# Attention over mixture memory, then an expert layer, on one core: first keys and queries through SyncE, both score parities in one step, 4096-byte stores

## The chip, the cores and the metric

One core of one Trainium2 chip. The metric is the device time of the kernel in microseconds. Of the engines, PE is TensorE (its weight loads are listed apart as PEld), DVE is VectorE, ACT is ScalarE, POOL is GpSimd and SP is SyncE. DMAs that POOL issues form the "software" queue, those that SP issues the "hardware" queue; both run on the core's 16 DMA engines.

## The reference

```
q, k, v: [8, 8, 576, 64] (batch, head, position, head_dim);  phi: [8, 8, 576, 32];  all f32
a      = softmax of phi over its 32 memories
k_m    = sum over positions of a * k      (32 x 64 for each batch and head);  v_m likewise with v
scores = q k_m^T / 8;  attn = softmax of scores over the 32 memories;  out = attn v_m
x      = out as [4608, 512]: a row is a position of a batch, heads side by side
y      = max(x w1_dense, 0) w2_dense                             (512 -> 512 -> 512)
       + gate * max(x w1[e], 0) w2[e],  e = argmax of x w_gate over 8 experts,  gate = softmax's value at e
```

The output is [4608, 512] f32.

## The kernel before, in words

The kernel works through eight batches of 576 rows. All matmuls are f16 with f32 sums in PSUM. Its 128 partitions hold a pair of heads (`a` is the parity of the head, `p` a position group of 64), so a tile such as `q` or `kv` has four pairs `j`, nine positions `t` of a group, and 64 elements. The keys, values and queries are read as f32 from memory and become f16 on the way by a DMA that POOL issues (`Lk`, `Lv`, `Lq`, L181 and L188). `phi` stays f32 and comes by SP (`Lphi`, L164, and in halves `Lphi0`, `Lphi1`, L173).

For each batch the steps are: `e0`, `e1` (exp of phi, ACT, L300); `z`, `rz` (its sums over positions); `kv` (72 matmuls that sum keys and values together, L333), `kvm` (division, L344), `T` (turned by matmuls), `kTc` and `vTc` (copied out of PSUM); `q0`, `q1` (queries turned by 72 matmuls each pair, L390), `qT0`, `qT1` (copied, L114); `s0`, `s1` (scores of one head parity each, eight matmuls of 288 columns, L412); `ET0`, `ET1` (exp, ACT, L425); `Z0`, `Z1` (sums over the 32 memories, spread back by a matmul with a block matrix, L436); `ln`, `inv` (logarithm and exp of its negative, ACT); `A0`, `A1` (the attention weights, DVE, L463). The value sums are never applied to the rows. They are multiplied into the first expert weights instead: `fd` and `fe` (L596) give 256 x 512 matrices, copied by `vd` and `ve`, and `hd` and `he` (L609) multiply A by them, for the dense and the expert half.

One expert per batch is chosen from the mean of the batch: `vg`, `pc`, `choose` (DVE, L501 to L507) write its number to `ei`, and POOL reads it, which is the start of `w1` (L211) and `w2` (L218), the loads of that expert's weights. `L`, `mxeq`, `ex`, `gates`, `pg`, `gB` give each row its gate, zero for rows that want another expert. `Hd` and `He` (L650 to L663) apply max and gate; `yd` and `ye` (L683) are the second matrices, both into one PSUM tile; `Y` (L707, L709) copies it to SBUF and `o` (L718, L723) stores it through SP, 128 rows at a time with 2048 bytes to a partition, the last 64 rows in two column halves. If any row wants another expert than its batch's, `others` adds it at the end, behind a branch.

The order of the work is written out by hand. The string `ORDER` lists every step as `name:batch`, with `/A`, `/V` or `/P` for the engine of a copy; the function `go` calls the steps in that order, and each engine's instructions stand in its queue in that order. [...]

Buffers are named tiles in pools with a fixed count: `q8`, `kv8`, `phi8` three each, `w1e`, `w2e` two each, `y` four (`NKEEP`), `qT`, `ET`, `lnz` one. In PSUM, `big` holds two tiles of two banks (`p_kv`, `p_q`, `p_s`, `p_z`, `p_h`, `p_g`), `one` three of one bank (`p_vw`, `p_y`), `sml` one.

Of the kernel before, what the change touches and what calls it, by code (L numbers as in the profile page):

```python
# [10 lines left out]
F32 = mybir.dt.float32  # L11
F16 = mybir.dt.float16
# [19 lines left out]
q1:3 He1:1 Lk:3 yd4:1 ye4:1 Lv:3 q0:3 Lphi:3 choose:2 A0:2 ye0:1 A1:2 ye1:1 L:2 Y4:1/A qT1:3/A
Y0:1/A ex:2 Y1:1/V mxeq:2 qT0:3/V hd1:2 yd3:1 yd2:1 e0:3 hd3:2 w1:2 ye3:1 e1:3 z:3 Hd1:2/A Hd3:2/A
gates:2 kv:3 pg:2 ye2:1 rz:3 gB:2/A kvm:3 Y3:1/A T:3 hd0:2 kTc:3/V w2:2 s1:3 Hd0:2/A fe:2 Y2:1/V
vTc:3/V Lq:4 ve1:2/V ET1:3 ve0:2/A hd2:2 s0:3 fd:3 Hd2:2/V vg:3 ET0:3 he2:2 He2:2 Z0:3 vd0:3/A yd0:2
ln0:3 vd1:3/V he0:2 he3:2 He0:2 yd1:2 He3:2 vgc:3 he1:2 Z1:3 pc:3 Lphi:5 Lphi:4 yd4:2 Lphi:6 He1:2
e0:5 ye4:2 inv0:3 e0:4 ye0:2 choose:3 ln1:3 q0:4 q1:4 inv1:3 A0:3 Y4:2/A e1:4 A1:3 Lk:4 qT1:4/V
qT0:4/V yd2:2 Y0:2/A L:3 ex:3 yd3:2 hd2:3 ye3:2 hd0:3 mxeq:3 ye2:2 gates:3 Hd2:3/V pg:3 Hd0:3/V z:4
e1:5 Y3:2/A gB:3/V rz:4 Y2:2/A Lv:4 w1:3 kv:4 kvm:4 hd1:3 hd3:3 T:4 e1:6 Hd1:3/A fe:3 ve1:3/V
kTc:4/V Hd3:3/A ye1:2 ve0:3/A Y1:2/A he3:3 he1:3 vTc:4/V He3:3 vg:4 fd:4 Lk:5 w2:3 He1:3 s1:4 yd4:3  # L40
ET1:4 vgc:4 vd1:4/A s0:4 ET0:4 vd0:4/V Lq:5 pc:4 he0:3 He0:3 yd3:3 Z0:4 ln0:4 inv0:4 he2:3 yd2:3
Lv:5 He2:3 A0:4 choose:4 Z1:4 ye2:3 ye3:3 ln1:4 q1:5 inv1:4 Lq:6 q0:5 A1:4 L:4 Y3:3/A qT1:5/V ex:4
mxeq:4 yd0:3 ye4:3 gates:4 qT0:5/A Y4:3/A kv:5 z:5 pg:4 e0:6 rz:5 yd1:3 kvm:5 gB:4/A T:5 kTc:5/A
Y2:3/V hd0:4 s1:5 ye1:3 ET1:5 vTc:5/V Hd0:4/V Z1:5 vg:5 s0:5 ln1:5 Y1:3/V w1:4 fe:4 hd3:4 ET0:5
ve1:4/V Z0:5 ye0:3 Hd3:4/V vgc:5 ln0:5 hd2:4 ve0:4/V hd1:4 o4:3 Hd2:4/A fd:5 pc:5 Y0:3/A Hd1:4/V
he0:4 He0:4 he3:4 yd0:4 inv1:5 vd0:5/A he2:4 He3:4 he1:4 Lv:6 w2:4 Lk:6 He2:4 o0:3 choose:5 He1:4
inv0:5 vd1:5/A yd1:4 yd2:4 A0:5 A1:5 w1:5 q1:6 q0:6 Lq:7 w2:5 ye2:4 qT0:6/A L:5 qT1:6/V mxeq:5 o3:3
o1:3 ye0:4 ex:5 kv:6 o2:3 Y2:4/V Y0:4/A z:6 rz:6 kvm:6 gates:5 hd1:5 yd3:4 yd4:4 T:6 hd3:5 ye1:4
Hd1:5/V kTc:6/V o2:0 vTc:6/A Y1:4/V hd2:5 Hd3:5/A ye4:4 o0:0 o1:0 Lphi:7 Y4:4/V s0:6 vg:6 vgc:6
Hd2:5/A s1:6 ET0:6 fe:5 pc:6 ET1:6 o3:0 ve0:5/V hd0:5 Lv:7 Lk:7 pg:5 Hd0:5/V choose:6 ve1:5/A gB:5/A  # L50
ye3:4 Z1:6 he0:5 ln1:6 yd0:5 Z0:6 He0:5 ln0:6 inv0:6 e1:7 e0:7 inv1:6 he1:5 Y3:4/V He1:5 yd1:5 he3:5
he2:5 He3:5 He2:5 yd3:5 q1:7 q0:7 A0:6 A1:6 ye3:5 ye0:5 qT1:7/V L:6 Y3:5/A ye1:5 yd2:5 ex:6 ye2:5
qT0:7/A mxeq:6 gates:6 z:7 w1:6 pg:6 Y1:5/A w2:6 Y0:5/V rz:7 fd:6 kv:7 Y2:5/A gB:6/A vd1:6/A yd4:5
vd0:6/V kvm:7 hd3:6 T:7 fe:6 ve1:6/V Hd3:6/A hd2:6 hd1:6 ye4:5 ve0:6/A Hd2:6/A kTc:7/A vTc:7/A o1:5
Hd1:6/V he1:6 hd0:6 o2:1 vg:7 fd:7 He1:6 vgc:7 s1:7 Y4:5/A pc:7 Hd0:6/A he2:6 o3:1 o0:2 o0:1 ET1:7
vd0:7/V He2:6 yd2:6 s0:7 he0:6 o0:4 o1:2 o4:1 vd1:7/A yd0:6 ET0:7 o3:4 o2:4 choose:7 o1:1 o4:4 He0:6
he3:6 He3:6 Z1:7 yd3:6 ln1:7 ye0:6 Z0:7 ye3:6 inv1:7 ln0:7 Y0:6/A inv0:7 Y3:6/V A1:7 A0:7 ye2:6 o3:5
o3:6 w1:7 yd1:6 ye1:6 L:7 Y2:6/A hd3:7 yd4:6 ex:7 hd2:7 Y1:6/A fe:7 w2:7 Hd3:7/A hd1:7 mxeq:7 o4:2
o0:5 o1:6 o0:6 o2:5 Hd2:7/A o4:5 gates:7 pn:0 hd0:7 ye4:6 Hd1:7/A ve1:7/V ve0:7/V pg:7 Y4:6/V o1:4
Hd0:7/A he0:7 gB:7/A He0:7 yd3:7 he3:7 he1:7 He3:7 yd2:7 he2:7 yd0:7 He1:7 He2:7 ye0:7 ye3:7 o4:6  # L60
Y0:7/A yd1:7 ye1:7 Y1:7/A ye2:7 Y3:7/V yd4:7 o3:2 o2:6 o2:2 ye4:7 Y2:7/A o0:7 o3:7 o1:7 o2:7 Y4:7/A
o4:7/A flags:0
# [4 lines left out]
def kernel(  # L67
# [28 lines left out]
    chunks = [(c, 0) for c in range(0, S - 127, 128)]  # L96
    if S % 128:
        chunks.append((S - 128, 128 - S % 128))
    NCH = len(chunks)
# [22 lines left out]
    A = [keep.tile([128, 2, S], F16, name=f"A{b}") for b in range(B)]  # L122
# [3 lines left out]
    em = [keep.tile([128, 1], F32, name=f"em{b}") for b in range(B)]  # L126
    e_i = [keep.tile([1, 1], I32, name=f"ei{b}") for b in range(B)]
# [5 lines left out]
    iota8 = const.tile([128, NCH, E], F32)  # L133

    steps = {}
# [13 lines left out]
    def input_tile(b, what):  # L149
        x = st[b]  # L150
        if what == "phi":
            x["phi"] = inp.tile([128, NJ, T, M], F32, tag="phi8", name="phi8")
        elif what == "q":
            x["q"] = inp.tile([128, NJ, T, Dh], F16, tag="q8", name="q8")
        elif "kv" not in x:
            x["kv"] = inp.tile([128, 2, NJ, T, Dh], F16, tag="kv8", name="kv8")
# [4 lines left out]
    @step("Lphi")  # L161
    def _(b, i, e):
        input_tile(b, "phi")
        nc.sync.dma_start(  # L164
            out=st[b]["phi"].rearrange("p j t m -> p j (t m)"), in_=rows(phi[b])
        )
# [11 lines left out]
    def _(b, i, e):  # L178
# [4 lines left out]
        )  # L183

# [24 lines left out]
    def expert_w1(e):  # L209
        w1e = wk.tile([128, DT, F], F16, tag="w1e", name="w1e", bufs=2)  # L210
        nc.gpsimd.dma_start(  # L211
            out=w1e, in_=moe_w1[ds(e, 1)].rearrange("o (dt p) f -> p (o dt) f", p=128)
        )
        return w1e

    def expert_w2(e):
# [299 lines left out]
    @step("w2")  # L516
    def _(b, i, e):
        st[b]["w2"] = expert_w2(st[b]["ev"])
# [344 lines left out]
```

## Time and profile before

| what | value |
|---|---|
| median of 3 runs | 174.44 us (172.74 to 174.59) |
| profiled execution: time, span | 171.97 us, 170.3 us |
| TensorE busy, granted clock | 143.5 us (84%), 0.996 |
| DVE, ACT, POOL busy | 101.0, 88.3, 32.2 us |
| read, written | 51.92 MB, 9.44 MB |
| software queue, hardware queue | 23.60 MB, 14.11 MB |
| last matmul ends | 164.45 us |

The bytes of a queue are counted as they are written, so the software queue, which turns f32 into f16, reads twice what it is listed with. Lines of the profile name an operation by its line in the kernel, its engine, and output and input tiles. In a chain or timeline the first number is the start and the second the duration, in microseconds. In a list of waits the numbers are the total, how many, and the longest.

### The profile page before, as it was taken

The page shows a single profiled execution, that of the slowest core. Times are in us where ns is not written, and L with a number is a line of the kernel's source. Part 1 is how long each engine was busy: PE and PEld are TensorE (multiplying, and loading weights), DVE is VectorE, ACT ScalarE, POOL GpSimd, SP SyncE. Part 2 cuts the span into 40 slices and gives each one's busy share as a digit, 9 for nine tenths or more (in the row PEclk, how much of TensorE's full clock was granted, in tenths as well). Part 3 has the DMA queues.
Part 4 walks back from the last instruction along what each step waited for, and adds up shares of the span by engine and source line. Part 5 has one row for each costly group of instructions (what it writes and reads, how often), then busy time and mean ns, then how long its engine had stood idle before and what let it go on. Part 6 is the DMA issues. An engine that isn't in the chain of part 4 may idle for free.

```text
span 170.3 us, 5557 instructions
## 1 busy us (share of the span) xinstructions
PE 143.5 (84%) x2401; PEld 84.8 (50%) x2401; DVE 101.0 (59%) x268; ACT 88.3 (52%) x153; POOL 32.2 (19%) x49
## 2 busy tenths in 40 slices
PE   4013779898999998999999989999699999999960
PEld 3012446465545655556655735565365655456430
DVE  0055275474795863688577856877477756476410
ACT  3130296887236665773666755443574674853130
POOL 7700009002600080008200600080030001200000
PEclk9999999999999999999999999999999999999998
DMA  4999999999999999999999999999999996899461
GB/s 121 300 235 209 206 207 195 205 204 208 199 207 219 246 332 228 243 207 174 203 206 209 187 201 212 289 365 237 208 208 207 259 386 251 111 229 396 190 224 45
DMA packets 32342, 38.18 MB, mean 224 GB/s; under 512 B 1588, under 2 KB 28212, under 8 KB 32312
## 3 DMA queue, kind: packets, MB, share of 16 engines
q0 software_dynamic: 22176, 23.60, 83.6%
q1 hardware_dynamic: 10056, 14.11, 24.0%
q8 instruction: 20, 0.33, 0.7%
q10 hardware_dynamic: 80, 0.07, 0.1%
q14 instruction: 10, 0.08, 0.1%
HBM read 51.92 MB, written 9.44 MB: 360 GB/s over the span
## 4 chain that ended last, share of the span: by engine, by line
PE 54%; DMA 30%; DVE 4%; issue 3%; POOL 2%; ACT 1%; POOLq 1%
PE p_y L683 26%; DMA w1e<-in_moe_w_dram 15%; PE p_h L609 14%; DMA kv<-in_k_dram 8%; DMA w2e<-in_moe_w_dram 7%; PE p_vw L596 3%; PE p_z L436 2%; PE p_s L412 2%; PE p_kv L333 2%; DVE HTe L663 1%; POOL q L188 1%; PE p_g L576 1%; DVE A L463 1%; PE p_q L390 1%; POOLq L513 1%
## 5 line engine op out<-in xcount | busy, mean ns | idle before, releaser
L683 PE MATMUL p_y<-w2d,HTd 128*128 128x512 f16 (+1 forms) x192 | 37.3, 346 | 0.0
L683 PE MATMUL p_y<-w2e,HTe 128*128 128x512 f16 (+1 forms) x192 | 36.7, 345 | 0.6 <-DMA w2e<-in_moe_w_dram 0.6
L663 DVE SCALAR_TENSOR_TENSOR HTe<-p_h,gB 128x576 f16<-128x576 f32 x32 | 23.5, 755 | 12.5 <-PE p_h L609 11.9
L211 POOL DMA_DIRECT2D w1e<-in_moe_w_dram x8 | 6.0, 746 | 112.1 <-DVE A L463 56.0
L609 PE MATMUL p_h<-A,vwd 128*128 128x288 f16 x128 | 22.1, 299 | 0.9 <-DVE qT L114 0.9
L707 ACT ACTIVATE y<-p_y 128x512 f32<-128x512 f32 (+1 forms) x25 | 13.8, 554 | 15.8 <-PE p_y L683 15.2
L683 PEld LDWEIGHTS <-HTe 128*128 128x128 f16 (+1 forms) x192 | 14.6, 101 | 13.7 <-issue 2.5
L683 PEld LDWEIGHTS <-HTd 128*128 128x128 f16 (+1 forms) x192 | 15.1, 101 | 11.6 <-issue 1.3
L609 PE MATMUL p_h<-A,vwe 128*128 128x288 f16 x128 | 19.5, 286 | 0.2 <-DVE HTd L652 0.2
L650 ACT ACTIVATE HTd<-p_h 128x576 f16<-128x576 f32 x21 | 13.4, 649 | 10.2 <-PE p_h L609 8.2
L300 ACT ACTIVATE E<-phi 128x576 f16<-128x576 f32 x16 | 10.5, 679 | 10.2 <-DMA phi<-in_phi_dram 9.5
L609 PEld LDWEIGHTS <-vwe 128*128 128x128 f16 x128 | 11.9, 97 | 5.8 <-issue 1.1
L609 PEld LDWEIGHTS <-vwd 128*128 128x128 f16 x128 | 11.3, 100 | 6.9 <-issue 2.4
L449 ACT ACTIVATE lnz<-p_z 128x576 f32<-128x576 f32 x16 | 10.3, 649 | 8.4 <-PE p_z L436 7.3
L709 DVE TENSOR_SCALAR y<-p_y 128x512 f32<-128x512 f32 (+1 forms) x15 | 9.5, 635 | 7.6 <-PE p_y L683 7.1
L425 ACT ACTIVATE ET<-p_s 128x576 f16<-128x576 f32 x16 | 10.2, 650 | 6.4 <-PE p_s L412 6.4
L114 DVE CAST vwe<-p_vw 128x512 f16<-128x512 f32 x12 | 8.0, 688 | 8.3 <-PE p_vw L596 8.3
L463 DVE TENSOR_TENSOR A<-ET,lnz 128x576 f16<-128x576 f16 x16 | 11.5, 744 | 0.3
L458 ACT ACTIVATE lnz<-lnz 128x576 f32<-128x576 f32 x16 | 10.7, 685 | 0.2
L114 ACT COPY qT<-p_q 128x1152 f16<-128x1152 f16 x7 | 7.7, 1114 | 4.1 <-PE p_q L390 4.1
L333 PE MATMUL p_kv<-kv,E 64*32 64x128 f16 x576 | 6.8, 232 | 3.1 <-DMA kv<-in_k_dram 3.1
L652 DVE TENSOR_SCALAR HTd<-p_h 128x576 f16<-128x576 f32 x11 | 8.3, 755 | 1.9 <-PE p_h L609 1.7
(86 smaller groups left out, 174.6 us busy)
## 6 DMA issues: line engine op xcount, KB each, us to landing
out_dram<-y SPq DMA_DIRECT2D x32, 256.0 KB, 4.8
q<-in_q_dram POOLq DMA_DIRECT2D x8, 576.0 KB, 12.1
kv<-in_v_dram POOLq DMA_DIRECT2D x8, 576.0 KB, 16.2
kv<-in_k_dram POOLq DMA_DIRECT2D x8, 576.0 KB, 14.3
w1e<-in_moe_w_dram POOLq DMA_DIRECT2D x8, 512.0 KB, 7.1
w2e<-in_moe_w_dram POOLq DMA_DIRECT2D x8, 512.0 KB, 11.6
phi<-in_phi_dram SPq DMA_DIRECT2D x7, 576.0 KB, 9.6
out_dram<-y SPq DMA_DIRECT2D x15, 64.0 KB, 4.2
```

Of the source, the lines that this page charges most:

```text
L114: (nc.scalar.copy if e == "A" else nc.vector.tensor_copy)(out=out, in_=in_)
L300: nc.scalar.activation(out=x["E"][:, :, hs].rearrange("p t j m -> p j t m"), in_=x["phi"][:, hs], func=AF.Exp,)
L333: nc.tensor.matmul(x["kvz"][M * j : M * j + M, a, 0 : 2 * Dh], lhsT=x["E"][rs, t, j], rhs=x["kv"][rs, :, j, t], start=(t == 0), stop=(t == ...
L425: nc.scalar.activation(out=st[b]["ET"][:, a].rearrange("m (p t) -> m p t", t=T), in_=st[b].pop(("ps", a)).rearrange("m (t p) -> m p t", t= ...
L449: nc.scalar.activation(out=st[b]["lnz"][:, a].rearrange("p (h c) -> p h c", h=2), in_=st[b].pop(("pz", a))[:, :, 0:HC], func=AF.Ln,)
L458: nc.scalar.activation(out=lnz, in_=lnz, func=AF.Exp, scale=-1.0)
L463: eng.tensor_mul(out=A[b][:, a], in0=st[b]["ET"][:, a], in1=st[b]["lnz"][:, a])
L609: nc.tensor.matmul(p_h[:, h, 0:HC], lhsT=vw[:, g, 128 * ft : 128 * ft + 128], rhs=a[:, g, HC * h : HC * h + HC], start=(g == 0), stop=(g = ...
L650: nc.scalar.activation(out=o, in_=p_h, func=AF.Relu)
L663: nc.vector.scalar_tensor_tensor(out=x["HTe"][:, ft].rearrange("p (h c) -> p h c", h=2), in0=x.pop(("pe", ft))[:, :, 0:HC], scalar=0.0, in ...
L683: nc.tensor.matmul(p_y[n * u : n * u + n, 0:w], lhsT=HT[:, ft, lo : lo + n], rhs=w2[:, ft, w * u : w * u + w], start=(half == 0 and ft == ...
L707: nc.scalar.activation(out=o, in_=p_y, func=AF.Copy, scale=1.0 / SC)
```

## The change

The first batch's keys and queries come through SP as f32, in halves (`Fk`, `Fq`), into a buffer of the `y` kind, and are made f16 on chip by DVE, ACT or POOL (`Ck`, `Cq`). Batch 0's key sums (`kk`, `kmk`, `Tk`) are steps of their own, apart from the value sums (`vv`, `kmv`, `Tv`). The step `s` issues the 16 score matmuls of both parities with the two parities side by side. Rows are cut in pairs: a chunk `c` of 128 rows takes every second row of 256, so that a partition holds two neighbouring rows and a store sends 4096 bytes from it.

Beside that, every batch gets its own slot for its expert's two weight matrices (`W1`, `W2`) in place of two buffers in turn, A has two buffers in place of eight, `phi8` two in place of three, and phi of later batches is issued by POOL (`/P`) with one exception. The gate weights' small PSUM tile moves from `sml` to `one`, there are 56 warming matmuls at the start in place of 16, and the whole order is written anew. Steps for using an expert's weights again (`rl`, `cw1`, `cw2`, and what `REUSE` guards) are defined and not used: `REUSE` is False. `others` computes A again, since A is no longer kept.

```diff
 ORDER = """
-ciota:0 Lphi:2 Lphi:1 cones:0 Lphi1:0 Lq:0 cid:0 Lwg:0 Lv:0 warm:0/8 warm:0/8 e1:1 wgt:0 Lphi0:0
-wgm:0 ciotac:0 wgc:0 Lk:0 e1:0 q1:0 q0:0 e0:0 qT0:0/V qT1:0/V z:0 kv:0 rz:0 cblk:0 kvm:0 Lw1d:0 T:0
-kTc:0/A vTc:0/V Lq:1 s0:0 fd:0 s1:0 ET0:0 Z0:0 ET1:0 ln0:0 vg:0 Z1:0 vd1:0/V inv0:0 ln1:0 vd0:0/V
-vgc:0 pc:0 choose:0 q1:1 q0:1 A0:0 qT0:1/V Lv:1 inv1:0 e0:1 Lk:1 A1:0 hd2:0 qT1:1/A Hd2:0/A L:0
...
-Y0:7/A yd1:7 ye1:7 Y1:7/A ye2:7 Y3:7/V yd4:7 o3:2 o2:6 o2:2 ye4:7 Y2:7/A o0:7 o3:7 o1:7 o2:7 Y4:7/A
-o4:7/A flags:0
+ciota:0 Lv:0 cones:0 Fk1:0 Lphi0:0 Lphi1:0 Lw1d:0 Lwg:0 Lq:1 Fk0:0 e0:0 wgt:0/V Ck0:0/V e1:0 Fq1:0
+z:0 warm:0/8 warm:0/8 warm:0/8 warm:0/8 warm:0/8 warm:0/8 warm:0/8 cid:0 Ck1:0/A Fq0:0 Lphi:1/P kk:0
+wgm:0 rz:0 ciotac:0 Cq1:0/P wgc:0 kmk:0 q1:0 Tk:0 Cq0:0/V vv:0 kTc:0/A qT1:0/A kmv:0 q0:0 Lv:1 Lk:1
+Tv:0 qT0:0/V s:0 ET0:0 vTc:0/V cblk:0 ET1:0 vg:0 Z0:0 vgc:0 ln0:0 Z1:0 pc:0 fd:0 q0:1 vd1:0/V inv0:0
...
+Lq:3 w2:1 Lk:3 Hd3:1/V kTc:2/A s:2 vg:2 ve0:1/V vgc:2 ve1:1/A fd:2 ET0:2 ET1:2 he3:1 pc:2 He3:1
...
+yd3:7 Y1:7/V flags:0 o0:6 o4:0 ye3:7 yd4:7 ye4:7 Y4:7/V Y2:7/A Y3:7/A o0:7 o1:7 o4:7/A
 """
...
-    chunks = [(c, 0) for c in range(0, S - 127, 128)]
-    if S % 128:
-        chunks.append((S - 128, 128 - S % 128))
-    NCH = len(chunks)
+    NP = S // 256
+    NCH = 2 * NP + 1
+    REM = S - 256 * NP
+    cols = [slice(256 * (c // 2) + c % 2, 256 * (c // 2) + 256, 2) for c in range(2 * NP)]
+    cols.append(slice(S - 128, S))
...
-    A = [keep.tile([128, 2, S], F16, name=f"A{b}") for b in range(B)]
+    W1 = keep.tile([128, B, DT, F], F16)
+    W2 = keep.tile([128, B, FT, D], F16)
...
-            x["phi"] = inp.tile([128, NJ, T, M], F32, tag="phi8", name="phi8")
+            x["phi"] = inp.tile([128, NJ, T, M], F32, tag="phi8", name="phi8", bufs=2)
...
-        nc.sync.dma_start(
+        (nc.gpsimd if e == "P" else nc.sync).dma_start(
             out=st[b]["phi"].rearrange("p j t m -> p j (t m)"), in_=rows(phi[b])
         )
...
+    @step("Fk0", "Fk1", "Fq0", "Fq1")
+    def _(b, i, e):
+        if ("f", i[1]) not in st[b]:
+            st[b]["f", i[1]] = wk.tile([128, NJ, T * Dh], F32, tag="y", name="f" + i[1], bufs=NKEEP)
+        src = dict(k=k, q=q)[i[1]]
+        hs = slice(2 * int(i[2]), 2 * int(i[2]) + 2)
+        nc.sync.dma_start(out=st[b]["f", i[1]][:, hs], in_=rows(src[b])[:, hs])
+
+    @step("Ck0", "Ck1", "Cq0", "Cq1")
+    def _(b, i, e):
...
+        if e == "P":
+            nc.gpsimd.tensor_copy(out=o, in_=st[b]["f", i[1]][:, hs])
+        else:
+            copy(e, out=o, in_=st[b]["f", i[1]][:, hs])
...
-    @step("kv")
-    def _(b, i, e):
+    def sums(b, u, w):
         x = st[b]
-        x["kvz"] = big.tile([128, 2, 512], F32, tag="big", name="p_kv")
+        if "kvz" not in x:
+            x["kvz"] = big.tile([128, 2, 512], F32, tag="big", name="p_kv")
         for t in range(T):
             for j in range(NJ):
                 for a in range(2):
                     rs = slice(64 * a, 64 * a + 64)
                     nc.tensor.matmul(
-                        x["kvz"][M * j : M * j + M, a, 0 : 2 * Dh],
+                        x["kvz"][M * j : M * j + M, a, Dh * u : Dh * (u + w)],
                         lhsT=x["E"][rs, t, j],
-                        rhs=x["kv"][rs, :, j, t],
+                        rhs=x["kv"][rs, u : u + w, j, t],
                         start=(t == 0),
                         stop=(t == T - 1),
                     )
...
+    @step("kv", "kk", "vv")
+    def _(b, i, e):
+        sums(b, *dict(kv=(0, 2), kk=(0, 1), vv=(1, 1))[i])
...
+    @step("s")
+    def _(b, i, e):
+        for a in range(2):
+            p_s = big.tile([128, 2, 512], F32, tag="big", name="p_s")
+            st[b]["ps", a] = p_s.rearrange("p h c -> p (h c)")[:, 512 - HC : 512 + HC]
+        for n in range(2):
+            for a in range(2):
+                for j in range(NJ):
+                    r = (j % 2) ^ a
+                    rs = slice(64 * r, 64 * r + 64)
+                    cs = slice(HC * (n ^ r), HC * (n ^ r) + HC)
+                    nc.tensor.matmul(
+                        st[b]["ps", a][M * j : M * j + M, cs],
+                        lhsT=st[b]["kT"][rs, a, j // 2],
+                        rhs=st[b]["qT"][rs, j // 2, a, cs],
+                        start=True,
+                        stop=True,
+                    )
...
+        if "A" not in st[b]:
+            st[b]["A"] = wk.tile([128, 2, S], F16, tag="A", name="A", bufs=2)
...
     @step("w2")
     def _(b, i, e):
-        st[b]["w2"] = expert_w2(st[b]["ev"])
+        load_w2(W2[:, b], *st[b]["ev"])
...
                 nc.tensor.matmul(
                     p_L[:, c],
-                    lhsT=A[b][:, a, c0 : c0 + 128],
+                    lhsT=st[b]["A"][:, a, cols[c]],
                     rhs=vg[:, a],
...
-    @step(*(f"o{c}" for c in range(NCH)))
+    @step(*(f"o{c}" for c in range(NP)))
     def _(b, c, e):
...
+        nc.sync.dma_start(
+            out=out[S * b + 256 * c : S * b + 256 * c + 256].rearrange("(p i) d -> p (i d)", i=2),
+            in_=st[b]["y"][:, 2 * D * c : 2 * D * c + 2 * D],
+        )
```

## The prediction

> **What bounds the kernel now.** I read first the top of the page (busy shares, the span in 40 slices), then the busy times by stage, then the chain that ended last in order of time, then what TensorE waited for, and the DMA queues in the first stage.
>
> ```profile
> span 170.3 us, 5557 instructions
> PE 143.5 (84%) x2401; PEld 84.8 (50%) x2401; DVE 101.0 (59%) x268; ACT 88.3 (52%) x153; POOL 32.2 (19%) x49
> ...
> PE   4013779898999998999999989999699999999960
> ...
> DMA  4999999999999999999999999999999996899461
> ...
> HBM read 51.92 MB, written 9.44 MB: 360 GB/s over the span
> ```
>
> Two resources are full at once. The DMA row is at 9 from the second slice (4 us) to about 140 us. PE is empty for its first slices and then at 9.
>
> ```profile
> 0.00:20.00 20.00, 5.90 (x195) 4.95 (x199) 5.99 (x20) 3.60 (x5) 6.18 (x14) 1.00 1.03 215
> 20.00:40.00 20.00, 17.37 (x370) 10.32 (x363) 12.13 (x35) 15.83 (x27) 4.45 (x6) 1.00 1.21 204
> 40.00:140.00 100.00, 95.85 (x1654) 56.62 (x1654) 69.46 (x180) 56.93 (x102) 20.04 (x27) 1.00 1.18 235
> 140.00:165.00 25.00, 24.41 (x194) 12.95 (x185) 13.37 (x36) 11.92 (x21) 1.48 (x2) 1.00 0.82 235
> ```
>
> The columns are the stretch, its length, PE, PEld, DVE, ACT and POOL busy, the granted clock, the DMA share, GB/s. PE stands idle 14.1 us of the first 20, 2.6 of the next 20, then only 4.2 in 100 us and 0.6 in the last 25; after 165 us there is only the last store (5.3 us). So PE is the bound from 20 us on, with the DMA close behind, and the first 20 us are a pure wait for input. The chain says for what:
>
> ```profile
> 3.69 13.47 DMA kv<-in_k_dram
> 17.30 1.21 PE p_kv L333 x62
> ...
> 19.79 0.67 PE p_s L412 x8
> 20.46 0.54 PE p_vw L596 x8
> 21.00 0.48 PE p_s L412 x8
> 21.48 0.59 PE p_z L436 x2
> ...
> 87.48 0.32 PE p_s L412 x8
> 87.80 0.56 PE p_y L683 x8
> 88.35 0.36 PE p_s L412 x8
> ...
> 90.22 0.25 PE p_z L436 x2
> ```
>
> The first keys land at 17.16 us, scores start at 19.79. The same step takes 0.67 and 0.48 us there and 0.32 and 0.36 later; Z takes 0.59 against 0.25. TensorE's waits later on are few:
>
> ```profile
> PE p_vw L596 <- DMA w1e<-in_moe_w_dram: 3.1, 3, 1.5
> PE p_kv L333 <- DMA kv<-in_k_dram: 3.1, 1, 3.1
> PE p_s L412 <- issue: 0.8, 1, 0.8
> ```
>
> [...] From 6 to 11 us [...], 567 packets against 559:
>
> ```profile
> q0 software_dynamic: 567, 0.63, 73.7%
> q1 hardware_dynamic: 559, 0.62, 43.0%
> ```
>
> [...] The granted clock on the page is 1.00 throughout[...]. [...] 72 matmuls of 128 columns took 0.73 us, 10 ns each.
>
> **The change part by part.** The sum is against the profiled execution: span 170.3, time 171.97, so 1.7 around the span. The median of the runs shown is 174.44, 2.5 above.
>
> (1) First inputs. Before, SP's queue begins with phi of batches 2, 1 and 0 (1.77 MB), and the page shows it alone from 2.8 us to about 5.8 at 389 GB/s (1.17 MB); then POOL's queue starts, whose q, v and k come in that order. Source bytes until k has landed: 1.77 + 3 x 1.18 = 5.3 MB. After, SP's order is Fk1 (half the keys, 0.59 MB), phi:0 in halves (0.295 each), gate weights, Fk0, Fq1, Fq0; POOL's is v:0, w1d, q:1, phi:1, v:1, k:1. The f32 copies cost no extra bus time: the cast queue moves about 206 GB/s written, 412 read, the plain one 389, so a transfer is priced by its f32 bytes. Fk1 and phi:0 fit in the 1.17 MB that move before POOL's queue starts. Then both queues send 2304-byte packets in turn, so each gets half of some 395 GB/s: Fk0 ends at 5.8 + 0.59/0.197 = 8.8, Fq1 at 11.8, Fq0 at 14.8, v:0 at 11.8; a landing is 0.8 later (5.3 MB worked out this way ends at 16.3, seen at 17.16): 9.6, 12.6, 15.6, 12.6.
>
> (2) Casts. wgt (two of 1.22 us on DVE, L258) stands ahead of Ck0 on DVE; its weights now come at about 7 instead of 9.66, so it ends by 9.7. Ck0 is 1152 f32 per partition: no row; between 0.75 (the 1152-element COPY of qT, L114)[...] so I take 0.8: keys at 10.6. Ck1 on ACT is free by 9 at 1.11 us (qT on ACT). Cq1 on POOL has no row either[...]; I take 2, ready at 14.7. Queued behind it on POOL are the issues of v:1 and k:1; POOL's DMA queue then still holds w1d, q:1 and phi:1 until about 20 us, which hides that. Cq0 on DVE: 15.6 + 0.8 = 16.4.
>
> (3) Keys apart from values. kk, kmk, q1, Tk, vv, kmv run in the gaps before q:0; they add 72 matmuls (0.7 us) in time when PE is idle anyway. On the path: q0 transposes 16.5 to 17.3, qT0 0.76 on DVE, s:0 at 18.2 to 18.5, against 19.79: **1.3 us** less. Bounds: 2.2 less with the fast ends, 0.7 more if the hardware queue gets less than its half (two fifths give Fq0 at 18 us).
>
> (4) Warm TensorE. The 16 early matmuls become 56, issued from about 8 us to 12-14, and later gaps are below 2 us. From s0 to the end of Z took 3.1 us before; warm, with s 0.4, two ET of 0.65, Z 0.3 and hand-overs of 0.3, about 2.3: **0.8 us** less (0 if the clock falls back). Loads agree: the bytes ahead of k:1 fall from 9.9 to 9.3 MB, 1.5 us, and choose:0 moves by 1 to 2, which moves w1:0.
>
> (5) Scores of both parities in one step. Before, four matmuls of 288 columns run at a time, twice, per parity: 0.32 + 0.36 us. After, eight at a time, twice: 0.24 us of streaming plus the lead-in, say 0.38. Saved 0.3 us x 8 batches = **2.4 us** of PE, between 0 (if eight don't overlap, or PE waits) and 2.7. The cost: s takes both of the two `big` PSUM buffers, so Z, hd, he and q of any batch wait for ET0 (0.65 us) and ET1 behind it on ACT. The cover in the new order is vg, fd and vgc, sometimes an expert part: 0.12 + 0.34 us and up. I take the left-over as equal to today's (L412 waits and the 0.8 us hole at 50.7).
>
> (6) 4096-byte stores, rows in pairs: the L and p_y weights are read with a step of two elements. [...] at worst L's ten loads double, 0.23 x 8 = 1.8 us; p_y's (98 ns) stay under its 215-ns matmuls even doubled. Stores already move at 388 GB/s. The last store is of 512 KB instead of 64 to 256: 0.7 us more transfer, partly beside the last matmuls: **+0.3** (0 to 1).
>
> (7) Own slots for every expert, A in two buffers, phi in two and on POOL's queue. The w1e issues come 1.25 to 1.5 us after `ei` (23.75 to 25.26, 40.26 to 41.51), so they wait for the choice, not for a buffer: nothing gained. phi adds eight issues of 0.77 us to POOL, which is idle 112 us ahead of w1e: nothing, unless a phi wait blocks q, k, v behind it.
>
> (8) The rest of the order is written anew; the page can't price that. I take the later PE holes (2.6 + 4.2) as they are, +-2 us.
>
> Sum: 170.3 - 1.3 - 0.8 - 2.4 + 0.3 = 166.1; with 1.7 around it 167.8; that is 0.976 of 171.97, and of the median 170.3.
>
> **The rivals.** *A, the DMA is the bound* (0.20). 61.4 MB at 390 GB/s are 157 us, begun at 2.8, and the row is full until 140. Then the earlier start (1.5 us for k:1) is kept, but PE's saving becomes waits on w1e and kv: 1.5 - 0.3 = 1.2 less, median 173.2. Against it: DMA share is 0.82 after 140, and PE's DMA waits are only 3.1 us after the start. *B, slower: both score buffers* (0.20). One mechanism: after s, PE has nothing without a `big` buffer and waits ET0 out, 0.85 us, and part of ET1. At 0.9 us in each of 8 batches it is 7.2 us: span 166.1 + 7.2 = 173.3, median 177.6. It decides from 0.5 us per batch on (8 x 0.5 = the 4.1 gained). For it: ACT is at 52% and in order, so ET can be late; against: vg, fd, yd and ye need no `big` buffer. *C, more* (0.12): the new order also closes most of the 6.8 us of holes: 4 more, median 166. *My forecast* has 0.48, 168.3 to 172.6.
>
> **How the numbers follow.** No change can be told from within 1%, 172.7 to 176.2. Faster: forecast 0.46, C 0.12, some of A: 0.61. Same: the rest of A and a little of B: 0.19. Slower: B, 0.20. The range 166 to 177.5 leaves out half of C and the worse half of B.
>
> **What would show it.** Right: first p_s near 18.4 us at about 0.4 us for 16, Z at 0.25 from the start, k:1 landing near 27; PE busy near 141 plus 3 for the new early matmuls; holes after 20 us near 7. Wrong: p_z waiting for ET (B), p_vw and p_kv waiting for DMA above 6 us (A), Cq1 over 3 us or Fq0 landing after 17, L loads above 150 ns. A reordering that delays one of the late choices would upset all of it.

## The result, and the profile after

The change made the kernel slower: 181.57 us (median of 4 runs, 180.43 to 185.22) against 174.51 (4 runs of before, 172.74 to 174.86); the ratio is 1.040, with a 95% interval of 1.030 to 1.051. I had forecast 170.3 us and a range up to 177.5. Some executions of one and the same program are two or three per cent longer than its others; ratios and means here leave those out on both sides, medians and lists of times do not. The means of before beside the later experiments are shorter (172.5 to 173.1 us) than its mean here (174.16), so ratios of different sets are not compared to a per cent; against those means the change, with 181.19 us in the mean, stands at about 1.05.

The profiled execution took 180.97 us, 1.7 of it outside the span. The top of its page:

```profile
span 179.3 us, 5776 instructions
...
PE 149.8 (84%) x2513; PEld 91.0 (51%) x2513; DVE 95.9 (53%) x260; ACT 94.2 (53%) x165; POOL 36.3 (20%) x54
...
PE   0095476889998999999979499999999999999950
...
PEclk9999655569999999999999969999999999999996
DMA  5999993999999999999999999999997799999461
...
HBM read 51.92 MB, written 9.44 MB: 342 GB/s over the span
```

The same bytes are moved as before, and the DMA row is no fuller. Three things differ: PE is busy 6.3 us more (149.8 for 143.5), the PE row has dents that before did not have (slices 5 to 7 and slice 23), and the granted clock is at half behind each of them. The busy times by stage, with the columns of the table before, say when the time is lost:

```profile
0.00:20.00 20.00, 6.81 (x240) 6.35 (x248) 5.37 (x14) 4.98 (x6) 6.55 (x14) 0.97 1.00 250
20.00:40.00 20.00, 15.37 (x346) 9.58 (x344) 10.01 (x35) 10.90 (x18) 5.20 (x7) 0.52 0.99 172
40.00:140.00 100.00, 95.03 (x1643) 56.66 (x1641) 61.26 (x167) 64.12 (x116) 22.75 (x31) 0.98 1.11 217
140.00:165.00 25.00, 24.82 (x288) 14.51 (x264) 15.38 (x35) 12.98 (x24) 1.79 (x3) 1.00 1.07 282
```

By 40 us before had done all but 120.3 us of its PE work, and after still has 127.7 us to do. In the later stages PE is idle 5.0 and 0.2 us, about as before (4.2 and 0.6). So most of the loss is made by 40 us. The chain of waits, start and duration in microseconds, shows where:

```profile
3.27 11.12 DMA fq<-in_q_dram
...
14.45 1.15 POOL q L205
...
16.31 0.23 PE p_kv L355 x30
16.54 3.36 issue
19.90 0.55 PE p_kv L355 x40
...
21.94 0.69 PE p_s L468 x16
...
23.36 1.18 PE p_z L491 x4
...
89.87 0.38 PE p_s L468 x16
...
99.83 0.64 PE p_kv L355 x61
100.46 2.92 issue
103.38 0.29 PE p_kv L355 x11
```

Twice TensorE stops for 3 us in the middle of a row of sums whose operands are all there. "Issue" means that it waited for nothing that the profile shows. The first such hole stands ahead of the first scores, which come at 21.94 us; I had said 18.2 to 18.5, and before had them at 19.79. After it the same 16 matmuls take 0.69 us, where they take 0.38 at 89.87: the clock fell. The trace has the granted clock full from 12.0 to 18.85 us, half to 39.3, full to 104.2, half to 107.6, then full to 175.9. Before had it full from 29.06 to 169.0. (These are the trace's records of the clock; the page and the tables count the time ahead of the first record, at 12.0 us here and at 29.06 before, as full.) The waits name the same place:

```profile
PE p_kv L355 <- issue: 6.3, 2, 3.4
PE p_h L701 <- ACT ET L480: 0.9, 2, 0.7
...
PE p_z L491 <- ACT ET L480: 0.6, 1, 0.6
```

My slower rival, in which both score buffers hold TensorE up behind ET, shows here at 1.5 us in all, not 7. What the holes are is the question of the experiments.

**The theory I formed (F).** The trace lists, beside the data, packets of 16384 bytes on a queue named "instruction": 21 of them in the execution after the change, for its 5026 matmuls and weight loads. I took them as one for each 256 instructions of TensorE (64 bytes each, an estimate from these counts; a matmul and its weight load are two). The two holes lie a whole number of such blocks apart: after 447 and after 3257 matmuls and loads, 11 x 256 = 2816 but for 6 (instructions of TensorE that are neither count too, and some records can be missing). In the first, instruction 191 ran at 13.94 us, the last one before the hole, 446, at 16.35, a packet of 0.89 us began at 17.58, and TensorE went on at 19.90: 5.95 us from one block's start to the next. So F says: a block comes no sooner than some 6 us after the one before, and a stretch in which 256 instructions need less stalls. Before, the same 256 instructions were spread over 9.2 us (13.49 to 22.66), with the wait for keys among them. The change added 80 instructions of warm-up and 144 of separate sums at just that place. The rival (S) is that the holes come from a dependency of the new kernel: buffers, loads by SyncE, or the joint scores.

### The profile page after: what moved, and what is told of

It is laid out like the page before. It is cut to its first block, busy times and chain, and to the rows that moved or that the text cites. A ratio compares the mean times of both kernels' runs of the same rounds, so it can differ in the third digit from the quotient of the medians.

```text
span 179.3 us, 5776 instructions
## 1 busy us (share of the span) xinstructions
PE 149.8 (84%) x2513; PEld 91.0 (51%) x2513; DVE 95.9 (53%) x260; ACT 94.2 (53%) x165; POOL 36.3 (20%) x54
## 4 chain that ended last, share of the span: by engine, by line
PE 76%; DMA 6%; DVE 6%; issue 4%; ACT 2%; SPq 1%; POOL 1%
PE p_y L774 37%; PE p_h L701 20%; DMA fq<-in_q_dram 6%; PE p_kv L355 4%; PE p_z L491 3%; PE p_vw L688 3%; PE p_q L426 3%; PE p_g L668 2%; PE p_s L468 2%; PE p_att L617 1%; ACT ET L480 1%; DVE HTd L744 1%; PE p_att L333 1%; DVE vwd L114 1%; DVE A L520 1%
## 5 line engine op out<-in xcount | busy, mean ns | idle before, releaser
L774 PE MATMUL p_y<-W,HTe 128*128 128x512 f16 (+1 forms) x192 | 38.3, 356 | 0.0
L234 POOL DMA_DIRECT2D W<-in_moe_w_dram x8 | 6.0, 746 | 107.4 <-DVE HTe L755 32.8
L798 ACT ACTIVATE y<-p_y 128x512 f32<-128x512 f32 (+1 forms) x24 | 13.3, 562 | 23.7 <-PE p_y L774 22.1
L774 PEld LDWEIGHTS <-HTe 128*128 128x128 f16 (+1 forms) x192 | 15.1, 105 | 12.8 <-issue 2.1
L742 ACT ACTIVATE HTd<-p_h 128x576 f16<-128x576 f32 x20 | 12.8, 649 | 12.0 <-PE p_h L701 7.4
L744 DVE TENSOR_SCALAR HTd<-p_h 128x576 f16<-128x576 f32 x12 | 9.0, 756 | 10.6 <-PE p_h L701 7.7
L114 ACT COPY qT<-p_q 128x1152 f16<-128x1152 f16 x11 | 12.0, 1120 | 5.0 <-PE p_q L426 5.0
L480 ACT ACTIVATE ET<-p_s 128x576 f16<-128x576 f32 x16 | 9.5, 648 | 9.3 <-PE p_s L468 9.3
L504 ACT ACTIVATE lnz<-p_z 128x576 f32<-128x576 f32 x16 | 10.2, 649 | 6.9 <-PE p_z L491 6.8
L355 PE MATMUL p_kv<-kv,E 64*32 64x128 f16 (+1 forms) x648 | 7.9, 227 | 6.9 <-issue 6.3
L333 PE MATMUL p_att<-ones,E 128*128 128x2 f16 x72 | 3.0, 165 | 9.1 <-ACT E L322 9.1
```

Source lines behind the costliest of these rows:

```text
L114: (nc.scalar.copy if e == "A" else nc.vector.tensor_copy)(out=out, in_=in_)
L355: nc.tensor.matmul(x["kvz"][M * j : M * j + M, a, Dh * u : Dh * (u + w)], lhsT=x["E"][rs, t, j], rhs=x["kv"][rs, u : u + w, j, t], start=( ...
L480: nc.scalar.activation(out=st[b]["ET"][:, a].rearrange("m (p t) -> m p t", t=T), in_=st[b].pop(("ps", a)).rearrange("m (t p) -> m p t", t= ...
L742: nc.scalar.activation(out=o, in_=p_h, func=AF.Relu)
L744: nc.vector.tensor_scalar_max(out=o, in0=p_h, scalar1=0.0)
L774: nc.tensor.matmul(p_y[n * u : n * u + n, 0:w], lhsT=HT[:, ft, cs], rhs=w2[:, ft, w * u : w * u + w], start=(half == 0 and ft == 0), stop= ...
```

## The experiments

**1. Fewer instructions, twice.** Wide warm-up matmuls (four times the columns, a quarter of the instructions), alone and then with the keys and values of batch 0 summed jointly again:

```
-            nc.tensor.matmul(p_x[:, 0:128], lhsT=onesb, rhs=onesb, start=True, stop=True)
+            nc.tensor.matmul(          # e // 4 times
+                p_x.rearrange("p (r c) -> p r c", r=4), lhsT=onesb,
+                rhs=onesb.unsqueeze(1).to_broadcast([128, 4, 128]), start=True, stop=True)
second kernel, in ORDER as well:  kk:0 -> kv:0   kmk:0 -> kvm:0   Tk:0 -> T:0   vv:0 kmv:0 Tv:0 left out
```

> The kernel after, with each step of eight 128-column warming matmuls made two of 512 columns: the same array time, 84 PE instructions fewer ahead of the first keys. Theory F (fetch): PE's instructions come in blocks of 256 through the busy DMA engines, and the 3.4 us hole inside the value sums is the wait for the block that begins at PE instruction 447. Then the hole leaves the value sums (all 72 run in one go) and stands 84 instructions later, at the start of the transposes of q0 (PE instruction 447 again, from about 17 to 20 us), and the time stays at that of the kernel after, within 1%. Theory V (the value sums wait for their data or for the clock): the hole stays inside the value sums, or is gone and with it some 3 us of the time. Theory S (both score buffers, all batches): no change.

> The kernel after with wide warming matmuls and batch 0's keys and values summed together again (72 matmuls fewer): 228 PE instructions fewer ahead of the first scores, so that instruction 447 comes after them. Theory F: no hole over 0.7 us before 20 us, scores of batch 0 at 18.8 to 19.5 instead of 21.9, clock at full rate through the first stage, 4 to 7 us less than the kernel after (174 to 177 by the medians). Theory V: as the kernel after, since the values land at the same time. Theory S: at most 1 us less.

The first took 186.14 and 187.89 us, ratio 1.085 (1.075 to 1.095). The timeline of its TensorE:

```profile
16.95 0.75 PE L361 MATMUL p_kv<-kv,E 64*32 64x64 f16 x72
20.78 0.70 PE L432 MATMUL p_q<-ident,q 64*64 64x64 f16 x36 [3.08 <-issue]
```

The hole is still at instruction 446, but with 84 fewer ahead of them the value sums now run through unbroken and the query transposes after them stall, although nothing about those transposes was changed. That is a count, not a dependency. The second hole stayed at 3257. The time I had wrong: a third hole, 3.38 us, came up at instruction 3768 (120.27 us), again a whole number of blocks after 446 but for 6, with another fall of the clock. Which dense stretch a block boundary falls into matters, so that taking instructions out can also do harm.

The second took 173.81, 175.38, 178.10 and 178.16 us (mean 174.59, before beside it 172.47), where the change had taken 180.43 to 185.22. F had the time and the scores right. The first hole is gone and the scores come 2.7 us earlier than after the change:

```profile
14.52 0.80 PE L361 MATMUL p_kv<-kv,E 64*32 64x128 f16 x72
...
19.27 0.44 PE L474 MATMUL p_s<-qT,kT 64*32 64x288 f16 x16 [0.97 <-DVE qT L114]
```

F had the clock wrong: it was not full through the first stage, but at half from 20.9 to 31.1 us, for half as long as in the change. From 14 us to that fall TensorE had no gap over 0.97 us. Of the second hole 1.53 us is left, at instruction 3001, one block short of 3257 and in the same sums. Wide matmuls and joint sums came together here; joint sums alone were not run.

**2. The joint scores, undone and done alone.** The changed kernel with `s0` and `s1` as two steps at the place of `s`; and the kernel before with `s` in their place and nothing else.

```
changed kernel, in ORDER:  s:b -> s0:b s1:b
kernel before, in ORDER:   s0:b ... s1:b -> s:b   (all 16 matmuls in one step; with it ET, Z, ln where they came between)
```

> The kernel after with the 16 score matmuls in the old grouping, parity 0 and then parity 1, at the same place. Theory F (the start cost the time, the joint scores gain 0.3 us in each of 8 batches): 1 to 3 us slower than the kernel after. Theory S (holding both score buffers cost the time): 3 us or more faster, with p_z waiting less.

> The kernel before with the joint score step alone. Theory F: PE spends 0.3 us less in each batch; 1 to 2.5 us less than before (172 to 173.5). Theory S: 3 us or more slower than before, with TensorE waiting for ET ahead of p_z or p_h.

Apart: 181.6 to 183.0 us, ratio 1.058 (1.052 to 1.065), with both holes at the same instructions. So the joint scores don't cause them. Alone in the kernel before: 173.27, 176.54, 177.22 and 177.41 us, beside 172.47 for before in the mean. The joint step itself is as short as I priced it, but in the kernel before it brought nothing that can be seen. As the step also had to be moved against its neighbours to keep PSUM's two large buffers legal, the run doesn't say whether the step or its place took the gain back.

**3. The disputed cost by itself.** No work of the kernel, only its densest kind of matmul, 2880 times, first with idle DMA engines, then while inputs are loaded.

```
+    sums(16)                                     # 16 x 72 matmuls on constants, no transfer under way
+    for x in ld + ldc: nc.vector.tensor_copy(out=x[:, 0, 0:1], in_=acc[:, 0, 0:1])   # loads wait for it
+    ... q and k by nc.sync.dma_start, v by nc.gpsimd.dma_start
+    sums(24)
```

> This kernel leaves the whole computation out: it runs the 72 key and value sums of one batch 40 times on constant data, the first 16 times with no transfer under way, the other 24 times while q, k and v are loaded through SyncE's and GpSimd's queues, and stores constants. It measures the disputed cost by itself: how long TensorE takes for 256 instructions of the densest kind when its instruction blocks come through idle DMA engines, and through busy ones. Array time is 1.16 us for 72 of them in the kernel before (17.30 us there), so 128 matmuls with their loads are 2.1 us of array time. Theory F (blocks of 256 instructions fetched through the DMA engines set the pace): under load 5.5 to 6.6 us for 256 instructions, as after's holes showed, and with idle engines clearly less, 2 to 4 us. Rival S (the holes come from something in the kernel's own dependencies): 2.1 us for 256 in both phases, with no hole at multiples of 256.

The timeline of TensorE, with the idle time before each group in brackets:

```profile
24.02 1.91 PE L81 MATMUL acc<-kv,E 64*32 64x128 f16 x128 [1.55 <-issue]
27.75 1.91 PE L81 MATMUL acc<-kv,E 64*32 64x128 f16 x128 [1.82 <-issue]
31.75 1.91 PE L81 MATMUL acc<-kv,E 64*32 64x128 f16 x128 [2.09 <-issue]
...
45.68 1.91 PE L81 MATMUL acc<-kv,E 64*32 64x128 f16 x128 [4.29 <-issue]
51.87 1.91 PE L81 MATMUL acc<-kv,E 64*32 64x128 f16 x128 [4.29 <-issue]
58.07 1.91 PE L81 MATMUL acc<-kv,E 64*32 64x128 f16 x128 [4.29 <-issue]
64.27 1.91 PE L81 MATMUL acc<-kv,E 64*32 64x128 f16 x128 [4.29 <-issue]
```

Every group shown is exactly 128 matmuls, that is 256 instructions, and then comes a wait. The period is 6.20 us under load ((64.27 - 45.68) / 3) and 3.5 to 4.0 us with idle DMA engines (3.8 in the mean from 12.84 to 31.75 us), for 1.9 us of array time at the half clock that was granted from 11.4 us on. The trace also says where the load adds: in each period from 12.84 us on one packet stands between the start of a block and the next; it begins 3.9 us after that start under load and 1.1 to 1.7 us after it with idle engines, and TensorE goes on 1.2 to 1.6 us after its end in both. The page counts the blocks:

```profile
q8 instruction: 22, 0.36, 1.0%
```

F's price is measured: 24 ns per instruction under load (6.20 us / 256), 15 ns with idle DMA engines (3.8 us / 256). The 22 packets fit blocks of 256 as well: 2880 matmuls and as many loads are 22.5 of them. For matmuls this small the wait is longer than the work: 4.29 us to 1.91 us of array time in each period under load.

**4. The hole made in the kernel before, with a control.** The sums of batch 0 done four times over (432 more instructions, 3.5 us of array time); and eight wide matmuls at the same place (16 more instructions, 2.92 us).

```
first:   +        for _ in range(4 if b == 0 else 1):        # around the three loops of kv
second:  + ORDER: kv:0 wide:0/8 rz:0                         # 8 matmuls of 512 columns on constants
```

> The kernel before with the 72 sums of batch 0 done four times over (each overwrites the last): 432 more TensorE instructions right after 17.3 us, and 216 x 16 ns = 3.5 us of array time. Rival (array time alone counts): first scores at 19.79 + 3.5 = 23.3 us, no hole, clock as before, 172.5 + 3.5 = 176 us at most. Theory F: instruction 447 falls near 18.9 us and 703 some 2 us later, but a block takes 5.5 to 6.6 us from the crossing before, so there is a hole of over 3 us that begins at instruction 703 of TensorE; first scores at 25.5 to 28 us; the clock falls to half, or stays at half, for 10 to 20 us after it; 178 to 183 us.

> The control: the kernel before with 8 matmuls of 512 columns on constants after the sums of batch 0: about the same array time (14 such took 5.7 us in the run with wide warm-up matmuls, so 8 take 3.3 us) but only 16 more instructions. Theory F and the rival agree here on no hole at 703: first scores at 22.5 to 23.5 us, 173 to 176 us. If it, too, shows a hole of 3 us with a fall of the clock, instructions are not what matters, and F is wrong.

Both kept the kernel's other work as it is. The dense one took 181.83 and 183.28 us, ratio 1.057 (1.048 to 1.066), and the wide one 173.95 in the mean, ratio 1.005 (1.001 to 1.010). Their timelines, dense first:

```profile
19.26 1.91 PE L334 MATMUL p_kv<-kv,E 64*32 64x128 f16 x128 [0.32 <-issue]
25.18 0.93 PE L334 MATMUL p_kv<-kv,E 64*32 64x128 f16 x51 [4.01 <-issue]
...
27.42 0.67 PE L413 MATMUL p_s<-qT,kT 64*32 64x288 f16 x8 [0.36 <-ACT kT L114]
```

```profile
17.02 1.16 PE L345 MATMUL p_kv<-kv,E 64*32 64x128 f16 x72 [2.49 <-DMA kv<-in_k_dram]
18.11 2.92 PE L290 MATMUL p_x<-onesb 128*128 128x512 f16 x8
...
21.63 0.43 PE L424 MATMUL p_s<-qT,kT 64*32 64x288 f16 x8 [0.36 <-ACT kT L114]
```

About the same array time costs 1 us as wide matmuls and 9.6 as small ones (mean 182.56 against 172.96 of before; 8.2 of the 9.6 us lie within the span). A hole of 4.0 us opens after 701 instructions (703 was written down ahead, one block after 447), in a kernel that has none of the change in it. The scores come at 27.42 us, and the clock is not full until 36.8 us instead of 29.06. Part of the 9.6 us is a second hole, 2.63 us at instruction 3512 with the clock at half from 108.5 to 111.9 us: the boundaries behind the addition had moved as well. Rival S has no room left for the first hole.

**5. The second hole thinned out.** In the changed kernel, output groups of earlier batches (`yd`, `ye`, few instructions of long duration) are put ahead of dense sums.

```
first:   z:6 kv:6 ... q1:6 kvm:6 q0:6  ->  z:6 kv:6 ... kvm:6 yd3:4 ye1:4 q1:6 q0:6
second:  mxeq:4 kv:5 z:5 rz:5 kvm:5  ->  mxeq:4 yd4:3 ye1:3 ye4:3 kv:5 z:5 rz:5 kvm:5 ... yd0:3 T:5
```

> The changed kernel with the dense stretch of batch 6 thinned out: two output matmul groups of batch 4 (16 instructions, 2.8 us) are put between the sums and the two query transposes of batch 6. Nothing else changes. Theory F: the hole of 3.14 us at instruction 3257 (100.24 us) shrinks under 1 us, the clock stays full from 40 us to the end, and the time falls by 2 to 4 us against the change, to 177 to 179.5 us (ratio to before 1.02 to 1.03). Rival (the hole there is a wait for a transfer or a buffer): it stays about where it is in time, 3 us long, and the time is 180 to 183 us.

> The run before moved the wrong batch's work: the hole at instruction 3257 lies in the sums of batch 5 (two query transposes, ten gate matmuls and the sums stand close there: 316 instructions in 4 us). Here the changed kernel is left as it is but for three output groups of batch 3 (2.1 us) put ahead of the sums of batch 5, and one more put after them. Theory F: instruction 3257 comes later by those 2 us, so that the hole there shrinks from 3.1 to 3.4 us to 0.5 to 1.7 us; the clock no longer falls to half at 104 us; 1.5 to 3.5 us less than the change, 178 to 180 us (ratio 1.025 to 1.04). Rival (a wait for a transfer or a buffer at that place): the hole stays 3 us, 180 to 183 us.

The first was a miss of mine: I had put the hole in batch 6, but its instructions belong to batch 5, so nothing ahead of 3257 was moved. Its hole stayed (3.21 us), and the time was that of the change, 180.9 to 183.0 us, ratio 1.057 (1.050 to 1.063). It serves as a control. The second moved the right work. These lines are of its execution of 181.5 us, both of the same step:

```profile
104.07 0.54 PE L355 MATMUL p_kv<-kv,E 64*32 64x128 f16 x41
105.81 0.41 PE L355 MATMUL p_kv<-kv,E 64*32 64x128 f16 x29 [1.19 <-issue]
```

The hole is down from 2.92 us in the chain to 1.2, and the trace shows no fall of the clock from 42.7 to 175.8 us. So the count of instructions sets this hole too. What it is worth in time is not shown. The three executions took 178.78, 181.50 and 181.75 us, the change 180.43 to 185.22, the control 180.92 to 183.00. The one of 181.50, whose hole had shrunk, was no faster than the change; its clock was at half from 18.8 to 42.7 us at the start. The one of 178.78 had a mean granted clock of 0.956 against 0.923 and 0.922 in the other two, so its gain can be that of the clock, and it has no trace to tell where.

**6. A version without holes.** Wide warm-up, joint sums in batch 0, the thinned sums of batch 5, and one more edit. In the change, `pg` writes the gates into every second column of PSUM, as its chunks are now the odd and even rows. Here they are written in a row, and the copy puts them in order:

```
-                p_g[:, S - REM : S] if skip else p_g[:, cols[c]],
+                p_g[:, S - REM : S] if skip else p_g[:, 128 * c : 128 * c + 128],
...
+            out=st[b]["gB"][:, 0:w].rearrange("p (c k i) -> p c k i", k=128, i=2),
+            in_=p_g[:, 0:w].rearrange("p (c i k) -> p c k i", i=2, k=128),
```

The same version was also run with the first keys and queries through GpSimd's queue again, in place of SyncE and the casts (`Fk`, `Ck`, `Fq`, `Cq` out, `Lk:0 Lq:0` behind `Lv:0`).

> The version that theory F asks for: wide warm-up matmuls, joint key and value sums in batch 0, the sums of batch 5 thinned out as in the run beside this one, and the broadcast gates written to PSUM in a row and put in order by the copy that follows (in the change they are written at every second column, and one such matmul of 128 columns took 309 ns, 290 in the run with joint sums, for 214 before). Expected against that run with joint sums (173.8 to 175.4 us): 40 x 76 ns = 3.0 us less TensorE work at most, 1.6 at least as the spans there overlap; the gap of 1.75 us at 95.7 us under 1 us. F: 171 to 173.5 us, level with before (ratio 0.990 to 1.003). If the change's slowness had another cause besides the holes and the gates (the stores, the loads by SyncE, the joint scores), it stays over 174 us.

> The version beside this one with the first keys and queries loaded through GpSimd's queue as f16 again (value, key, query in that order; no casts on chip), to price that part of the change alone. My steps (1) to (3) say that SyncE's path brings the first scores 1.3 us forward (in truth 0.5 us: 19.27 us in the run with joint sums for 19.79 before): first scores at 19.8 to 21 us here and 0.5 to 1.5 us more than the version beside it. Rival (the first transfers are bound by the bytes, and the f32 path moves as many from memory): the same time within 0.5 us. If it is faster, SyncE's path is itself a loss.

The first took 173.84, 175.72, 176.58, 176.87, 178.43 and 178.70 us, ratio 1.019 (1.012 to 1.026), which is formed from the first two: better than the change, slower than before, and above the 171 to 173.5 us that I expected. It is level with the version with joint sums that it was made from. By what was written down ahead, a time over 174 us (174.78 in the mean) says that something besides the holes and the gates is left. No gap of TensorE over 1 us is left behind the first keys, and the gates cost what they cost before:

```profile
L674 PE MATMUL p_g<-ident,gm 128*128 128x128 f16 (+1 forms) x40 | 3.3, 214 | 0.6 <-DVE gm L665 0.6
```

In the changed kernel that row reads 5.5 us and 309 ns, in the version with joint sums (clock 0.957 there and here 0.956) 290 ns: writing every second column of PSUM costs 76 ns more in the mean of the 40 matmuls, and 1.7 us of busy PE (5.0 us there, 3.3 here; they overlap). This version's TensorE ends at 164.33 us, where before's ended at 164.41, but the span ends 7.8 us later, not 5.9.

With GpSimd's queue at the front: 175.0 to 177.3 us, ratio 1.016 (1.008 to 1.024), scores at 18.69 us for 18.92. The two can't be told apart, so no gain or loss of SyncE's path for the first keys and queries is to be seen. My expectations there (scores at 19.8 to 21 us, 0.5 to 1.5 us for the path) were wrong.

**7. Warm-up and the last stores.** The version of experiment 6 with 4 wide warm-up matmuls for 14; and with the rows of the last batch stored chunk by chunk in 2048-byte pieces.

```
first:   ORDER: warm:0/8 seven times -> twice
second:  ORDER: o0:7 o1:7 -> r0:7 ... r1:7 ... r2:7 r3:7, each behind its Y
+            out=out[r : r + 256].rearrange("(p i) d -> p i d", i=2)[:, c % 2],
+            in_=st[b]["y"][:, D * c : D * c + D],
```

> The version with joint sums, thinned sums in batch 5 and gates in a row, but with 4 wide warm-up matmuls (1.6 us) in place of 14 (5.7 us), to price the warm-up of the change by itself. There the clock was full from 13.7 to 20.6 us, then half to 30.8 us; before, with 16 small warm-up matmuls, it became full at 29.06 us and stayed so. Step (4) of my prediction (a warm TensorE at the front is worth 0.8 us, later gaps being too short to lose the clock): 0.5 to 1 us slower than the run with 14, 174.5 to 176.5 us where that took 173.8 and 175.7. Theory G (a warm-up that early is wasted, since TensorE idles from 16 to 20 us for data and loses the clock at 20.6 us, for 10 us and more): no full clock before 25 us, full by 30 us at the latest, first scores at 18.5 to 19.5 us as the sums start earlier, 172.5 to 174.5 us, and less spread among the runs.

> The version with joint sums, thinned sums and gates in a row, but with the rows of the last batch stored chunk by chunk in 2048-byte pieces again (256 KB each, as soon as its chunk is out of PSUM), not as two stores of 512 KB at the very end. In the version without that, TensorE ended at 164.33 us against 164.41 before, but the span ended 7.8 us after it, against 5.9 before: the last 64 KB store was issued at the same moment (164.83 us) behind 512 KB issued at about 164 us. Theory T (the last store waits in the queue behind the large one, so the larger stores cost 1.5 to 2 us at the end, where I predicted 0.3): 5.5 to 6.3 us from TensorE's end to the end of the span, 1.3 to 2 us less than 173.8 to 175.7 us, so 172 to 174.2 us. Rival (the end is set by something else, such as the landing of the last 64 KB alone): 7 us or more as before, and the same time within 0.5 us.

Fewer: 177.2 to 179.0 us, ratio 1.028 (1.022 to 1.034). Theory G falls: the clock was not full before 35.1 us, and fell once more at 55.6. Whether the early warm-up is worth more than the 0.8 us I gave it is not settled: by the means it is 3.1 us, by the medians of all executions 1.0 (177.74 against 176.72), and the next kernel, with all 14, lost its clock at the start for twice as long as the trace of the version it was made from (19.0 to 39.4 us against 20.6 to 30.8) and was as slow as this one.

Last stores: 177.6 to 179.0 us, ratio 1.034 (1.027 to 1.040). Theory T fell in this form: the span ended 9.4 us after TensorE instead of 7.8 (in an execution of 180.44 us), and the last store occupied SyncE for 1.84 us in place of 0.47. Taking the large stores apart in this way is no remedy. The other traces speak against the large stores too: the version with joint sums has the same ones, and its tail, from TensorE's end to the span's end, is 6.5 us, while the kernel before with joint scores, which keeps the 256 KB stores, has one of 7.8. What was last in the version of experiment 6 was TensorE. Its jump over `others`, at the end of the program, began at 165.32 us and took 5.85 us, to 171.17, when SyncE had been through since 170.03. The jump took 3.6 to 4.5 us in the ten traces whose tail is 5.5 to 6.5 us (before 3.89, the change 4.26), and 5.5 to 6.4 in the four whose tail is 7.5 us or more. In those four, two instruction packets came within 0.4 us of each other, one of them of 2.7 to 2.9 us. Why the jump took longer there was not tested.

## Why the prediction was wrong, step by step

**The step that failed is (3)**, "they add 72 matmuls (0.7 us) in time when PE is idle anyway", and with it the 56 warm-up matmuls in (4). I priced added matmuls by array time and looked only for idle array time to put them in. What was scarce there were instructions: 224 more of them stood ahead of the first scores, and a block's 256 now had 2.4 us (13.94 to 16.35) where before had spread them over 9.2. The hole cost 3.4 us, and the scores came at 21.94 us instead of 18.4; without it they came at 19.27 and 18.92, so that 2.7 to 3.0 us of the delay is the hole.

**(4) failed in itself as well.** The clock was full from 12.0 us on (before, from 29.06), but it fell at 18.85 us, in the hole, and was back at 39.3. It also fell without the hole, at 20.9 us in the version with joint sums and at 20.6 in that of experiment 6, and was back 10.2 us later. "Later gaps are below 2 us" held in both, with 0.97 us the longest gap from 14 us to the fall; that gaps so short would keep the clock was my estimate. What the trace of experiment 6 shows there is a TensorE that stood idle for 2.95 of the 4.8 us from 15.8 us to the fall, in four gaps of 0.61 to 0.97 us. How much time the half clock costs beside the hole was not measured apart. Joint sums with wide warm-up matmuls take the hole and half of the half-clock stretch back; in one set of runs, that version stood at 1.012 of before (174.59 against 172.47 in the mean), and the change with its scores apart, holes and all, at 1.058.

**(8)** hid the second one: the order puts transposes, gate matmuls and sums of batch 5 within 4 us. I had taken later holes as they are, +-2 us; this one is 2.9 us and is followed by 3.4 us at half clock. What it adds to the time is not shown (experiment 5).

**(6)** was mis-sized. I looked at what reads with a step of two and took it to cost nothing, an estimate: right for the output weights (346 ns before and 345 in the version with joint sums for a p_y matmul) and for the gate matmuls (167 and 167 ns). I overlooked what writes with a step of two, the 40 matmuls of `pg`, 2.1 us more in the changed kernel's profile (5.5 for 3.4). The last store was +0.3 in my sum; from TensorE's end (172.81 us, chain and timeline) to the span's end it took 6.5 us, before 5.9.

**(1) and (2)** were off in size. The first half of the keys that came second landed at 11.45 us (I said 9.6), the last queries at 17.3 (15.6), past the 17 us that I had named as a sign of being wrong; Cq1 on GpSimd took 1.15 us where I took 2, the casts on DVE 0.76 for 0.8, both estimates of mine. As the version with GpSimd's queue shows, the part bought nothing that can be seen. In (7) I counted eight phi issues on POOL; there are six.

**(5)** was right as an operation: 16 matmuls in 0.38 us at full clock, for 0.32 + 0.36 before, 0.3 us in each batch, and in the busy sum 4.2 us for 7.6. As time it was not to be seen: taking it out of the changed kernel gave 1.058, but the control of experiment 5, which has the joint scores, gave 1.057, and putting it into the kernel before gained nothing.

**Rival B**, which I had on the slower side, was the wrong mechanism (1.5 us seen). Rival A, the DMA bound, was not it either: PE's waits for transfers are 7.1 us in before's list of waits, and that of the change has none.

**What stays open.** The version without holes has TensorE end as early as before, though its array work is 1.5 us more (145.0 against 143.5, of which warm-up is 3.8), and still ends 1.8 us later, with TensorE's jump as the last to be done. Why the jump is longer there, why the joint scores' gain is missing, and what takes the clock at 20 us in the versions without the first hole were not brought to a cause. No version beat the kernel before.

## What to carry to other kernels

Price a small matmul by its instructions as well as by its columns: where 256 TensorE instructions (128 matmuls with their loads) stand in less than the 5.9 to 6.2 us that a block took here with busy DMA engines (6.20 in experiment 3, 5.92 in experiment 4), expect a stall at the block boundary, and count where the boundaries fall before adding or moving such matmuls. Eight wide matmuls at such a place made no hole, and long ones put ahead of such a stretch shrank one from 2.9 to 1.2 us. An "issue" wait in the middle of a uniform group, at the same instruction count in several kernels, is the sign; look at the granted clock behind it as well, in the trace's records.

## What the runs showed of the hardware that I had not expected

- TensorE's instructions come in 16 KB blocks of 256: in a row of small matmuls, one block per 6.20 us under full DMA load (share 1.09) and per 3.8 us with idle DMA engines (0.02), though the packet itself takes 0.9 to 1.3 us in both (experiment 3). The load lengthens the wait ahead of the packet, from 1.1 to 1.7 us to 3.9.
- After a hole of 2.9 to 3.4 us the granted clock was at half for 3.4 us (104.2 to 107.6) in one place and for 20.5 us (18.85 to 39.3) in the other; after one of 1.53 us (95.95 us in the version with joint sums) it stayed full. The length of the gap alone doesn't decide: in the kernel before with joint scores it was at half for 3.4 us after a gap of 1.9 us (103.1 us), and in the version of experiment 6 for 10.2 us with no gap over 0.97 us.
- At the end of the program TensorE's jump over a branch that was not needed took 3.6 to 6.4 us, and in the version of experiment 6 it was the last to be done.
- Matmuls that write up to 128 columns at every second column of PSUM took 290 ns in the mean, in a row 214.
- A copy of 1152 elements per partition from f32 to f16 took 0.76 us on DVE, 1.14 to 1.15 on GpSimd and 1.14 on ACT.
